# A cross network on one core: row products ordered from a table, sums that let tail reads pass, and a run that ends three tiles later in a split tile

## The chip, the cores and the metric

The kernel runs on one core of a Trainium2 chip. The metric is the time of one execution on the device, in microseconds. Before the change the median of three timed runs is 470.85 us (470.77 to 471.45).

## The reference

```python
B, F, D, L = 16384, 26, 16, 6          # Din = F * D = 416
x = x0                                  # (16384, 416), bfloat16
for l in range(L):
    proj = jnp.einsum('bd,de->be', x, ws[l]) + bs[l]
    x = x0 * proj + x                   # element by element
return x
```

Six layers follow each other. Each multiplies the batch with a 416 x 416 matrix, adds a bias, multiplies with the input x0 and adds its own input.

## The kernel before

**Tiling.** x is held transposed: features on the 128 partitions, batch along the free dimension. The batch of 16384 is cut into 8 groups (`g`) of 2048, a group into 4 chunks (`j`) of 512. The 416 features are three tiles of 128 (`t` as input, `i` as output) and a tail of 32. A *job* is a pair (g, l) of group and layer, 48 in all; `order` lists them so that several groups are under way at once. Work is put down in *items*: a "tile" is one output tile i of a job, for all four chunks; a "tails" item makes the 32 tail features of two or three jobs together (a *batch* of tails). A chunk of an output tile is one PSUM bank (128 x 512 in f32); there are eight banks, and `ring` holds the order in which they are handed out (`take`).

**Two forms of the same products.** A chunk of an output tile needs 3 x 128 + 32 rows of the contraction. `full` and `rows32` do that as three products over all 128 rows and one over a 32-row group. In the middle of the kernel, from item `s_lo` to `s_hi` (123 tiles, 14 batches of tails), `stream` does it otherwise: each 128-row product is cut into its four 32-row groups (`tile_position=(r * T32, 0)`), so that four products, on four row groups of the array and into four different banks, go side by side. A chunk then has 3 products on each row group and 1 more, its tail, on the group that `quad` gives: 13 in all, which is 13/4 of the array's time for one product. [...]

**What sets the order.** TensorE takes its queue in order, so the order of the row products decides how well the four row groups are filled. Before, `weave` finds it while the program is built: a beam search over states (when each row group is free, which chunks are in flight, when banks come free), with costs in units of one product: a hand-over 1.1, a bank back 1.1 + 2.85 + 0.8 after a chunk's last product, a tail read by VectorE 4.0, a change of array shape 0.45. At a batch of tails the row products stop, and `tails` is issued. Banks are taken from `ring` in turn (`held[c] = ring.pop(0)`). After the run the ring is turned to the rotation nearest to its state.

**Reading the banks.** `evacuate_chunk` has ScalarE add the bias and write a chunk to `tw` (L574). When both chunks of a pair are there, VectorE multiplies by x0 (L583) and adds the layer's input (L586), 1024 wide. `hold=True` and `release=True` let the recorder put a sum behind the next multiply, so that VectorE does not wait for itself. Of each batch of tails in the run, the second tail is read from PSUM by VectorE (L613), the others by ScalarE (L617); these are put down when `tails` is called, behind everything that VectorE's queue already holds. The tiles outside the run are read by `evacuate` (L539 on ScalarE, 1024 wide where two banks lie side by side; L548 and L553 on VectorE).

**Around the run.** The item ahead of the run is a full tile. The run ends ahead of tile 1 of job (6, 4), named `behind`; three more tiles, among them that one, follow in full form, in the modes FR and RF (first the full products and then the row products, or the other way), before the next batch of tails. The last job is made in natural layout (`nat_full`, L1122) and stored.

Of the kernel before, what the change touches and what calls it, by code (L numbers as in the profile page):

```python
# [3 lines left out]
P = 128  # L4
# [195 lines left out]
FENCE = 1.1  # L200
READ, SERVE, BACK = 1.1, 2.85, 0.8
SECOND = 4.0
CHANGE = 0.45


def weave(tails, events, width, slack=12):

    n = len(tails)
    size = [[3 + (r == tails[c]) for r in range(4)] for c in range(n)]
    rest = [[sum(size[c][r] for c in range(k, n)) for r in range(4)] for k in range(n + 1)]

    states = [(0.0, (0.0,) * 4, (), 0, (0.0,) * 4 + (4.6, 4.6, 9.3, 9.3), 8.5, 0, None, (0,) * 4)]
    for step in range(4 * n):  # L220
        found = {}
        for state in states:
            for due in (False, True):
                idle, free, flight, begun, banks, act, ev, log, last_ = state
                now = min(free)
                if due:
                    if ev == len(events) or begun < events[ev][0]:
                        continue
                    m = events[ev][1]
                    part = [(f - now + 1e-6) % 1.0 for f in free]  # L230
                    at = now + max(part)
                    if any((f - now + 1e-6) // 1.0 > v for f, v in zip(free, last_)):
                        continue
                    if len(banks) < m or any(banks[k] > at + 3 * k for k in range(m)):
                        continue
                    on = at + 3.25 * m + 3 * CHANGE
                    idle += sum(at - now - p for p in part)
                    moved = tuple(on + (f - now + 1e-6) // 1.0 for f in free)
                    flight = tuple((c, left, moved[r] if abs(end - free[r]) < 1e-9 else -9.0, r)
                                   for c, left, end, r in flight)  # L240
                    log = ((None, m, at, tuple(int((f - now + 1e-6) // 1.0) for f in free), on), log)
                    banks = list(banks[m:])
                    for k in range(m):
                        if k == 1:
                            banks.append(on - CHANGE - 1 + READ + SECOND + BACK)
                            continue
                        act = max(act, on - CHANGE - 1 + READ) + SERVE
                        banks.append(act + BACK)
                    banks = tuple(sorted(banks))
                    free, now, ev = moved, min(moved), ev + 1  # L250
                over = sorted((end, k) for k, (c, left, end, q) in enumerate(flight) if not left and end <= now)
                if over:
                    for end, k in over:
                        act = max(act, end + READ) + SERVE
                        banks += (act + BACK,)
                    banks = tuple(sorted(banks))
                    flight = tuple(f for f in flight if f[1] or f[2] > now)
                r = free.index(now)
                last = min(events[ev][0] + slack, n - 4) if ev < len(events) else n
                more = [(max(now, end + FENCE), k) for k, (c, left, end, q) in enumerate(flight) if left >> r & 1]  # L260
                if begun < last and banks:
                    more.append((max(now, banks[0]), None))
                if not more:
                    continue
                soon = min(s for s, k in more)
                for start, k in more:
                    if start > soon + 1.3:
                        continue
                    if k is None:
                        c, left = begun, 15  # L270
                    else:
                        c, left = flight[k][:2]
                    end = start + size[c][r]
                    left &= ~(1 << r)
                    fl = list(flight)
                    bk, sd = banks, begun
                    if k is None:
                        fl.append((c, left, end, r))
                        bk, sd = banks[1:], begun + 1
                    else:  # L280
                        fl[k] = (c, left, end, r)
                    fr = free[:r] + (end,) + free[r + 1:]
                    idl = idle + start - now
                    low = min(fr)
                    key = (tuple(round(10 * (f - low)) for f in fr),
                           tuple(sorted((lf, tails[x], max(-2, round(5 * (e - low)))) for x, lf, e, q in fl)),
                           sd, tuple(max(0, round(2 * (b - low))) for b in bk), ev)
                    if key not in found or found[key][0] > idl:
                        found[key] = (idl, fr, tuple(fl), sd, bk, act, ev, ((c, r, start, left), log),
                                      last_[:r] + (size[c][r],) + last_[r + 1:])  # L290

        def score(s):
            idl, fr, fl, sd = s[:4]
            own = list(rest[sd])
            age = 0
            far = 0.0
            for c, left, end, q in fl:
                age += sd - c
                chain = end
                for r in range(4):  # L300
                    if left >> r & 1:
                        own[r] += size[c][r]
                        chain += FENCE + size[c][r]
                far = max(far, chain)
            stop = max(f + w for f, w in zip(fr, own))
            return idl + 4 * max(stop, far) - sum(fr) - sum(own) + 0.15 * age + 0.5 * max(0, len(fl) - 6)

        states = sorted(found.values(), key=score)[:width]
        if not states:
            raise ValueError("no order found")  # L310
    best = min(states, key=lambda s: s[0] + 4 * max(s[1]) - sum(s[1]))
    log, entries = best[7], []
    while log:
        entries.append(log[0])
        log = log[1]
    out, latest, when = [], {}, 0
    for e in entries[::-1]:
        if e[0] is None:
            for r in range(4):
                for k in range(e[3][r]):  # L320
                    latest[r][-1 - k][0] = e[4] + e[3][r] - 1 - k
            out.append([e[2], -1, None, e[1]])
        else:
            c, r, start, left = e
            latest[r] = [[start + k, r, c, r] for k in range(size[c][r])]
            out += latest[r]
    out.sort(key=lambda x: (x[0], x[1]))
    return best[0] + 4 * max(best[1]) - sum(best[1]), max(best[1]), [(c, r) for t, o, c, r in out]


def bass_standalone__cross_network_dcn__recsys_kernel(
# [228 lines left out]
    tile_tw, tile_out = {}, {}  # L560

    def evacuate_chunk(g, l, i, j, b):
# [15 lines left out]
        a = j - j % 2  # L578
        if not {a, a + 1} <= out_:
# [3 lines left out]
        add("dve", lambda h: h.tensor_tensor(tw[r][:, o], tw[r][:, o], x0s[s0][:, c], ALU.mult),  # L583
            reads=[("tw", r, k) for k in both] + [x0_tok(s0, i, k) for k in both],
            writes=[("tw", r, k) for k in both], release=True)
        add("dve", lambda h: h.tensor_tensor(xs[so][:, c], tw[r][:, o], src(i, a, a + 2), ALU.add),  # L586
            reads=[("tw", r, k) for k in both] + [stok(i, k) for k in both],
            writes=[("x", so, i, k) for k in both], hold=True)
        if len(out_) == NJ:
            pr.flush()  # L590
            finish_tile(g, l)
# [94 lines left out]
    def tails(batch, corners_last=False):  # L686
        bs_ = take(len(batch))
# [13 lines left out]
        for (g, l), b in zip(batch, bs_):  # L701
# [21 lines left out]
        while later:  # L723
# [288 lines left out]
    def stream(run):  # L1012
# [10 lines left out]
        for c, r in order_:  # L1023
# [6 lines left out]
            if c not in held:  # L1030
                held[c], count[c] = ring.pop(0), 0
# [239 lines left out]
```

## Time and profile before

| | before |
|---|---|
| timed runs, median (lowest to highest) | 470.85 us (470.77 to 471.45) |
| profiled execution | 471.08 us |
| its span, first to last instruction | 469.3 us |
| TensorE clock granted | 1.000 of full speed |
| TensorE busy (PE) | 463.3 us, 7761 products |
| weight loads (PEld), beside PE | 268.9 us |
| VectorE (DVE) busy | 403.8 us, 700 instructions |
| ScalarE (ACT) busy | 378.8 us, 596 instructions |
| products in the run | 6396 (5904 from L1038 and 492 from L1042) |

A profile line gives the source line, the engine, the operation, what it writes and reads (output <- inputs), the shape, and the count; then busy time, mean length of one in ns, and the idle time of the engine just before, with what ended it. A timeline line gives the start and the length in us, and merges equal instructions that follow each other ("x12"): its length runs from the first start to the last end. Products overlap (each is shown from its start to its modelled end), so a group's busy time is less than count times length. PEld is TensorE's weight load, which stands in the same queue as the products.

### The profile page before, as it was taken

How to read it: one execution, taken by the hardware profiler on the slowest of the kernel's cores; microseconds unless marked ns; L12 is line 12 of the kernel's file. 1: busy time of each engine (PE TensorE's matmuls, PEld its weight loads, DVE VectorE, ACT ScalarE, POOL GpSimd, SP SyncE). 2: the span in 40 equal slices, each digit the busy share in tenths (PEclk: the TensorE clock that was granted, in tenths of full speed). 3: DMA queues.
4: the chain of work that ended last, by engine and by line, in shares of the span. 5: the costliest groups of instructions: out<-in, count | busy, mean ns of one | idle time of the engine just before them, and what ended most of it. 6: DMA issues, size and time to landing. Idle time of an engine off the chain costs nothing.

```text
span 469.3 us, 17315 instructions
## 1 busy us (share of the span) xinstructions
PE 463.3 (99%) x7761; PEld 268.9 (57%) x7761; DVE 403.8 (86%) x700; ACT 378.8 (81%) x596; POOL 7.3 (2%) x15
## 2 busy tenths in 40 slices
PE   9999999999999999999999999999999999999996
PEld 5444576665655557566666657565455665654442
DVE  2897988888889888988989899988989888988897
ACT  4687788787878788787988888888788887976775
POOL 1000000000000000000001000000000000000000
PEclk9999999999999999999999999999999999999999
DMA  8976878401002979094667993980000194128799
GB/s 224 187 158 129 157 130 168 64 3 26 2 3 40 175 187 148 20 150 148 115 114 114 235 150 71 177 252 3 25 2 3 26 147 148 36 48 185 153 170 290
DMA packets 139087, 53.75 MB, mean 115 GB/s; under 512 B 112763, under 2 KB 138501, under 8 KB 139013
## 3 DMA queue, kind: packets, MB, share of 16 engines
q1 hardware_dynamic: 138856, 52.54, 54.5%
q8 instruction: 60, 0.98, 0.9%
q14 instruction: 15, 0.11, 0.1%
q10 hardware_dynamic: 156, 0.11, 0.1%
HBM read 5.97 MB, written 13.63 MB: 42 GB/s over the span
## 4 chain that ended last, share of the span: by engine, by line
PE 93%; DVE 3%; ACT 1%; DMA 1%; issue 0%; DVEq 0%; ACTq 0%
PE ps L1038 68%; PE ps L659 7%; PE ps L1042 6%; PE ps L706 6%; PE ps L647 2%; PE ps L694 1%; DVE x L1186 1%; PE ps L680 1%; PE ps L778 1%; PE ps L796 1%; DVE x L1180 1%; DMA x<-x 1%; ACT tw L539 1%; DVE x L586 1%; DVE tw L583 1%; ACT tw L574 1%
## 5 line engine op out<-in xcount | busy, mean ns | idle before, releaser
L1038 PE MATMUL ps<-x,wm 32*128 32x512 bf16 x5904 | 353.2, 375 | 0.7 <-DVE ts L613 0.6
L574 ACT ACTIVATE tw<-ps,bias 128x512 bf16<-128x512 f32 x492 | 307.5, 687 | 41.5 <-PE ps L1038 26.4
L1038 PEld LDWEIGHTS ps<-x,wm 32*128 32x128 bf16 x5904 | 215.4, 92 | 125.1 <-PE ps L1038 3.4
L583 DVE TENSOR_TENSOR tw<-tw,x 128x1024 bf16<-128x1024 bf16 x246 | 167.4, 691 | 39.1 <-ACT tw L574 38.3
L586 DVE TENSOR_TENSOR x<-tw,x 128x1024 bf16<-128x1024 bf16 x246 | 159.6, 685 | 0.4
L1042 PE MATMUL ps<-x,w 32*128 32x512 bf16 x492 | 149.3, 374 | 0.0
L539 ACT ACTIVATE tw<-ps,bias 128x1024 bf16<-128x1024 f32 (+1 forms) x42 | 37.9, 970 | 15.2 <-PE ps L680 11.6
L1042 PEld LDWEIGHTS ps<-x,w 32*128 32x128 bf16 x492 | 42.3, 92 | 5.6
L659 PE MATMUL ps<-x,wm 128*128 128x512 bf16 x176 | 40.3, 380 | 0.0
L617 ACT ACTIVATE ts<-ps,bias 128x512 bf16<-128x512 f32 x33 | 21.0, 685 | 20.7 <-PE ps L694 20.7
L706 PE MATMUL ps<-x,wm 128*32 128x512 bf16 x564 | 33.6, 380 | 0.0
L548 DVE TENSOR_TENSOR tw<-tw,x 128x1024 bf16<-128x1024 bf16 (+1 forms) x39 | 24.3, 633 | 6.2 <-ACT tw L539 5.9
L659 PEld LDWEIGHTS ps<-x,wm 128*128 128x128 bf16 x176 | 16.2, 98 | 21.9 <-issue 3.6
L706 PEld LDWEIGHTS ps<-x,wm 128*32 128x32 bf16 x564 | 13.5, 96 | 17.6 <-ACT tw L574 3.2
L553 DVE TENSOR_TENSOR x<-tw,x 128x1024 bf16<-128x1024 bf16 (+1 forms) x39 | 23.1, 629 | 0.0
L621 DVE TENSOR_TENSOR x<-ts,x 128x512 bf16<-128x512 bf16 x47 | 18.3, 417 | 0.0
L613 DVE SCALAR_TENSOR_TENSOR ts<-ps,bias,x 128x512 bf16<-128x512 f32 x14 | 10.5, 749 | 6.3 <-PE ps L694 6.1
L619 DVE TENSOR_TENSOR ts<-ts,x 128x512 bf16<-128x512 bf16 x33 | 13.6, 416 | 0.0
L916 POOL COPY ost<-ot 128x512 bf16<-128x512 bf16 x6 | 5.9, 982 | 414.5 <-DMA ot<-x 414.5
L1122 PE MATMUL ps<-wm,x 128*128 128x416 bf16 x48 | 9.8, 340 | 0.0
L1174 ACT ACTIVATE x<-ps 128x416 bf16<-128x416 f32 x16 | 7.7, 517 | 2.1 <-PE ps L1122 2.0
L806 DVE COPY x<-ps 128x512 bf16<-128x512 bf16 x5 | 2.0, 422 | 8.3 <-PE ps L796 8.1
(50 smaller groups left out, 77.9 us busy)
## 6 DMA issues: line engine op xcount, KB each, us to landing
out_dram<-ost SPq DMA_DIRECT2D x6, 1664.0 KB, 7.9
x<-x SPq DMA_DIRECT2D x24, 96.0 KB, 2.2
x<-in_x_dram SPq DMA_DIRECT2D x8, 208.0 KB, 3.8
x<-in_x_dram SPq DMA_DIRECT2D x4, 416.0 KB, 7.8
out_dram<-ost SPq DMA_DIRECT2D x2, 832.0 KB, 5.4
wm<-in_ws_dram SPq DMA_DIRECT2D x5, 312.0 KB, 3.4
x<-x SPq DMA_DIRECT2D x22, 64.0 KB, 2.4
out_dram<-x SPq DMA_DIRECT2D x3, 416.0 KB, 4.4
```

Of the source, the lines that this page charges most:

```text
L539: add("act", lambda h, a=a, w=w, b0=b0: h.activation(tw[r][:, a * CH:(a + w) * CH], psum[:, b0 * CH:(b0 + w) * CH], ACT_F.Identity, bias=b ...
L548: add("dve", lambda h, a=a, e=e: h.tensor_tensor(tw[r][:, a * CH:e * CH], tw[r][:, a * CH:e * CH], x0s[s0][:, i * GC + a * CH:i * GC + e * ...
L553: add("dve", lambda h, a=a, e=e: h.tensor_tensor(xs[so][:, i * GC + a * CH:i * GC + e * CH], tw[r][:, a * CH:e * CH], src(i, a, e), ALU.ad ...
L574: add("act", lambda h: h.activation(tw[r][:, j * CH:(j + 1) * CH], bank(b), ACT_F.Identity, bias=bias[:, i, l:l + 1], scale=1.0), reads=[( ...
L583: add("dve", lambda h: h.tensor_tensor(tw[r][:, o], tw[r][:, o], x0s[s0][:, c], ALU.mult), reads=[("tw", r, k) for k in both] + [x0_tok(s0 ...
L586: add("dve", lambda h: h.tensor_tensor(xs[so][:, c], tw[r][:, o], src(i, a, a + 2), ALU.add), reads=[("tw", r, k) for k in both] + [stok(i ...
L617: add("act", lambda h: h.activation(ts[r][:, :], bank(b), ACT_F.Identity, bias=bias[:, 3, l:l + 1], scale=1.0), reads=[("ps", b), "bias"], ...
L621: add("dve", lambda h: h.tensor_tensor(x3s[so][:, :], ts[r][:, :], res, ALU.add), reads=[("ts", r)] + rtok, writes=[("x3", so), ("x3", so, ...
L659: add("pe", lambda h, t=t, j=j, k=k, w=w: h.matmul(bank(banks[j])[:, k * w:(k + 1) * w], wm[l][:, t, ecols], src(t, j, j + 1)[:, k * w:(k ...
L706: add("pe", lambda h, t=t, j=j, src=src, l=l, b=b, ro=ro, qo=qo: h.matmul(psum[qo, b * CH:(b + 1) * CH], wm[l][:, t, NT * P:D], src(t, j, ...
L1038: add("pe", lambda h, l=l, t=t, j=j, b=b, q=q, ecols=ecols, src=src, kw=kw: h.matmul(bank(b), wm[l][q, t, ecols], src(t, j, j + 1)[q, :], ...
L1042: add("pe", lambda h, l=l, b=b, q=q, ecols=ecols, s3=s3, kw=kw: h.matmul(bank(b), w3[l][q, ecols], s3[q, :], **kw), reads=tok3 + [("w3", l ...
```

## The change

1. **A table instead of the search.** `weave` is gone. `ORDER` is a string with one letter for each (chunk, row group) and a bar for each batch of tails; a letter says how many chunks ago the chunk was begun, and the row group. `replay` walks through it with its own costs (in twentieths of a product: hand-over 22, a bank back 70 after ScalarE's read begins, which is 19 after the last product's end, the next read 56 later, VectorE's tail bank 92, a change of shape 9), and from that fixes the start order of the single products, the bank of each chunk and the time at which each chunk is read. Bank numbers come from `replay`'s own list, which starts with banks 0 to 3 free at once, 4 and 5 at 92, 6 and 7 at 186, and no longer from `ring`.
2. **Sums yield.** `evacuate_chunk` makes two steps of a pair, `multiply` and `plus`. It keeps an estimate of when VectorE would be through (`dve`). If that lies past the end of the coming batch of tails (`phases`), the steps, and all that follow, go to `behind_tail`, and `tails` puts them down right after VectorE's own tail read, ahead of its work on the other tails.
3. **The run ends later.** `behind` is now tile 0 of job (7, 4), three tiles on, and belongs to the run. Of that last tile only the four tail products are row products in the run (`keep=NJ`, `part=0`); its twelve 128-row products follow right behind as full products, chunk by chunk, and each pair of chunks is read as soon as it is there. The other tiles keep their form.

```diff
-FENCE = 1.1
-READ, SERVE, BACK = 1.1, 2.85, 0.8
-SECOND = 4.0
-CHANGE = 0.45
-def weave(tails, events, width, slack=12):
...
+SLOT = 20
+FENCE, CHANGE = 22, 9
+READ, NEXT, BACK, SECOND, PAIR, TAILS = 19, 56, 70, 92, 56, 220
+LETTERS = "ABCDEFGHIJKLMNOPQRSTUVWXYZabcdefghijklmnopqrstuvwxyz0123456789"
+ORDER = (
+    "ABCDABaXOTUBCjUReLMhSHIVOTYBOIDhKAbJCQLVOEBXOQDNKADZOQXBOIDVCfMJSXYFOIDVCMXdSIHB|CXMRCPIBaDUZKTA"
...
+def replay(tails, events, keep, part):
...
+    size = [[(3 if c < n - keep else part) + (r == tails[c]) for r in range(4)] for c in range(n)]
+    free, flight, begun, act = [0] * 4, {}, 0, 170
+    banks = [(0, 0), (0, 1), (0, 2), (0, 3), (92, 4), (92, 5), (186, 6), (186, 7)]
...
+    for letter in ORDER:
+        if letter == "|":
...
+            for k, (_, b) in enumerate(got):
+                if k == 1:
+                    banks.append((on + SECOND, b))
                     continue
+                start = max(act, on - CHANGE + READ)
+                act = start + NEXT
+                banks.append((start + BACK, b))
...
+        age, r = divmod(LETTERS.index(letter), 4)
+        c, now = begun - age, free[r]
+        over(now)
+        if not age:
+            t, home[c] = banks.pop(0)
+            start, begun = max(now, t), begun + 1
+            flight[c] = [sum(1 << q for q in range(4) if size[c][q]), 0, r]
         else:
+            start = max(now, flight[c][1] + FENCE)
...
+        free[r] = start + SLOT * size[c][r]
...
     out.sort(key=lambda x: (x[0], x[1]))
...
-    def evacuate_chunk(g, l, i, j, b):
+    tile_tw, tile_out, ready = {}, {}, {}
+    phases, behind_tail, dve = [], [], [0]
+    def evacuate_chunk(g, l, i, j, b, read):
...
+        todo = [multiply, plus]
         if len(out_) == NJ:
-            pr.flush()
-            finish_tile(g, l)
+            todo.append(lambda: finish_tile(g, l))
+        while todo:
+            if behind_tail or phases and max(dve[0], ready[(g, l, i, a)]) + PAIR > phases[0] + 14:
+                behind_tail.extend(todo)
+                return
+            if len(todo) > 1 or len(out_) < NJ:
+                dve[0] = max(dve[0], ready[(g, l, i, a)]) + PAIR
+            todo.pop(0)()
...
-    def tails(batch, corners_last=False):
-        bs_ = take(len(batch))
+    def tails(batch, corners_last=False, banks=None):
+        bs_ = banks or take(len(batch))
...
                 evacuate_tail(*batch[k], bs_[k], vector=k == 1)
+                while behind_tail:
+                    behind_tail.pop(0)()
...
-    behind = ("tile", (LAST - 1, L - 2), 1)
+    behind = ("tile", (LAST, L - 2), 0)
...
-    def stream(run):
+    def stream(run, keep, part):
...
-            if c not in held:
-                held[c], count[c] = ring.pop(0), 0
...
-        at = list(ring)
-        turn = min(range(8), key=lambda k: max(at.index((k + i) % 8) - i for i in range(8)))
-        ring[:] = [(turn + i) % 8 for i in range(8)]
+        home = {c: b for _, r, c, b in plan if r >= 0}
+        ring[:] = sorted(left)
+        (g, l), i, _ = chunks[-1]
+        banks = [home[c] for c in range(len(chunks) - keep, len(chunks))]
...
+        full(g, l, i, banks, False, True, lambda j: j % 2 and evacuate(g, l, i, banks, [j - 1, j], 2),
+             ts_=range(part, NT))
+        ring.extend(sorted(banks))
...
-    s_lo, s_hi = items.index(("tile", (0, 2), 1)), items.index(behind)
+    s_lo, s_hi = items.index(("tile", (0, 2), 1)), items.index(behind) + 1
...
-            stream(items[s_lo:s_hi])
+            stream(items[s_lo:s_hi], NJ, 0)
```

More of the change, by code (lines that the diff above doesn't have):

```diff
@@ L197, in _ @@
                 run("dve", h)
-FENCE = 1.1
-READ, SERVE, BACK = 1.1, 2.85, 0.8
-SECOND = 4.0
-CHANGE = 0.45
-def weave(tails, events, width, slack=12):
-    n = len(tails)
[L216 to L263, printed above, removed]
-                    continue
[L265 to L322, printed above, removed]
-        else:
-            c, r, start, left = e
-            latest[r] = [[start + k, r, c, r] for k in range(size[c][r])]
-            out += latest[r]
@@ L327, in weave @@
     out.sort(key=lambda x: (x[0], x[1]))
-    return best[0] + 4 * max(best[1]) - sum(best[1]), max(best[1]), [(c, r) for t, o, c, r in out]
+    return out, read, [b for t, b in banks]
 def bass_standalone__cross_network_dcn__recsys_kernel(
@@ L578, in evacuate_chunk @@
         a = j - j % 2
+        ready[(g, l, i, a)] = max(ready.get((g, l, i, a), 0), read)
         if not {a, a + 1} <= out_:
@@ L582, in evacuate_chunk, with multiply, plus @@
         o, c = slice(a * CH, (a + 2) * CH), slice(i * GC + a * CH, i * GC + (a + 2) * CH)
[L583 to L588, printed above, removed]
-        if len(out_) == NJ:
-            pr.flush()
-            finish_tile(g, l)
+        def multiply():
+            add("dve", lambda h: h.tensor_tensor(tw[r][:, o], tw[r][:, o], x0s[s0][:, c], ALU.mult),
+                reads=[("tw", r, k) for k in both] + [x0_tok(s0, i, k) for k in both],
+                writes=[("tw", r, k) for k in both], release=True)
+        def plus():
+            add("dve", lambda h: h.tensor_tensor(xs[so][:, c], tw[r][:, o], src(i, a, a + 2), ALU.add),
+                reads=[("tw", r, k) for k in both] + [stok(i, k) for k in both],
+                writes=[("x", so, i, k) for k in both], hold=True)
+            if len(out_) == NJ:
+                pr.flush()
+        todo = [multiply, plus]
+        if len(out_) == NJ:
+            todo.append(lambda: finish_tile(g, l))
[6 more added lines that the diff above has]
+            todo.pop(0)()
     def evacuate_tail(g, l, b, vector=False):
@@ L1020, in stream @@
                 n += NJ
-        idle, end, order_ = weave([quad(g, l, j)[0] for (g, l), i, j in chunks], [(n, len(b)) for n, b in due], 400)
-        held, count, seen = {}, {}, {}
-        for c, r in order_:
-            if c is None:
-                tails(due.pop(0)[1], corners_last=True)
+        plan, read, left = replay([quad(g, l, j)[0] for (g, l), i, j in chunks], [len(b) for n, b in due],
+                                  keep, part)
+        phases.extend(on for _, r, _, on in plan if r < 0)
+        count, seen = {}, {}
+        for _, r, c, b in plan:
+            if r < 0:
+                dve[0] = max(dve[0], phases.pop(0)) + PAIR * len(behind_tail) + TAILS
+                tails(due.pop(0)[1], corners_last=True, banks=c)
                 continue
@@ L1029, in stream @@
                 start_job(g, l, ahead=False)
-            if c not in held:
-                held[c], count[c] = ring.pop(0), 0
-            b, q, ecols = held[c], slice(r * T32, (r + 1) * T32), slice(i * P, (i + 1) * P)
+            count[c] = count.get(c, 0) + 1
+            q, ecols = slice(r * T32, (r + 1) * T32), slice(i * P, (i + 1) * P)
             t = seen[c, r] = seen.get((c, r), -1) + 1
@@ L1035, in stream @@
             s3, tok3 = x3_src(g, l)
-            kw = dict(start=count[c] == 0, stop=count[c] == 4 * NT, tile_position=(r * T32, 0))
-            if t < NT:
+            kw = dict(start=count[c] == 1, stop=count[c] == 4 * NT + 1, tile_position=(r * T32, 0))
+            if t < (NT if c < len(chunks) - keep else part):
                 add("pe", lambda h, l=l, t=t, j=j, b=b, q=q, ecols=ecols, src=src, kw=kw: h.matmul(
```

68 lines of the change are left out of this document (62 added, 6 removed).

## The prediction

> **What bounds the kernel now.** I read the page's busy times first, then the chain that ended last, then the groups, and last the timeline at the run's two ends and across one batch of tail products.
>
> ```profile
> span 469.3 us, 17315 instructions
> PE 463.3 (99%) x7761; PEld 268.9 (57%) x7761; DVE 403.8 (86%) x700; ACT 378.8 (81%) x596; POOL 7.3 (2%) x15
> ...
> PE 93%; DVE 3%; ACT 1%; DMA 1%; issue 0%; DVEq 0%; ACTq 0%
> ```
>
> TensorE is busy for 99% of the span and carries 93% of the chain; VectorE and ScalarE have room. But "busy" hides something: in the run, four products on four 32-row groups of the array go side by side, and PE counts as busy when only one of them works. So the question is how many row-steps stand open.
>
> ```profile
> L1038 PE MATMUL ps<-x,wm 32*128 32x512 bf16 x5904 | 353.2, 375 | 0.7 <-DVE ts L613 0.6
> L574 ACT ACTIVATE tw<-ps,bias 128x512 bf16<-128x512 f32 x492 | 307.5, 687 | 41.5 <-PE ps L1038 26.4
> L583 DVE TENSOR_TENSOR tw<-tw,x 128x1024 bf16<-128x1024 bf16 x246 | 167.4, 691 | 39.1 <-ACT tw L574 38.3
> L586 DVE TENSOR_TENSOR x<-tw,x 128x1024 bf16<-128x1024 bf16 x246 | 159.6, 685 | 0.4
> L1042 PE MATMUL ps<-x,w 32*128 32x512 bf16 x492 | 149.3, 374 | 0.0
> L659 PE MATMUL ps<-x,wm 128*128 128x512 bf16 x176 | 40.3, 380 | 0.0
> L613 DVE SCALAR_TENSOR_TENSOR ts<-ps,bias,x 128x512 bf16<-128x512 f32 x14 | 10.5, 749 | 6.3 <-PE ps L694 6.1
> ```
>
> The end of the run, TensorE's timeline (start, length, what):
>
> ```profile
> 426.16 0.44 PE L1042 MATMUL ps<-x,w 32*128 32x512 bf16 x2
> 426.48 0.82 PE L1038 MATMUL ps<-x,wm 32*128 32x512 bf16 x3
> 427.14 0.37 PE L1042 MATMUL ps<-x,w 32*128 32x512 bf16 x1
> 427.44 2.76 PE L659 MATMUL ps<-x,wm 128*128 128x512 bf16 x12
> 430.14 0.61 PE L680 MATMUL ps<-x,w 32*128 32x512 bf16 x8
> 430.68 5.35 PE L659 MATMUL ps<-x,wm 128*128 128x512 bf16 x24
> ```
>
> Twelve full products take 2.76 us, the last of them 0.38, so one step is (2.76 - 0.38) / 11 = 0.216 us. A row product has the same 512 columns and the same step. The run's work is (5904 + 492) / 4 = 1599 steps, 345.4 us.
>
> One batch of tail products, again TensorE's timeline:
>
> ```profile
> 415.07 0.85 PE L1038 MATMUL ps<-x,wm 32*128 32x512 bf16 x10
> 415.85 2.12 PE L706 MATMUL ps<-x,wm 128*32 128x512 bf16 x36
> 417.91 0.42 PE L694 MATMUL ps<-x,w 32*32 32x512 bf16 x12
> 418.26 0.61 PE L1038 MATMUL ps<-x,wm 32*128 32x512 bf16 x7
> ```
>
> The last row product before it starts 0.375 before the end at 415.92, at 415.54, and has used its step by 415.76; the run goes on at 418.26. A batch takes 2.50 us, and there are 14 (L613, one a batch, has x14): 35.0 us. The new table has 14 bars, so this stays.
>
> The run's first rows, with ScalarE's reads beside them (the second of the two is shown once more by itself, from a narrower window):
>
> ```profile
> 37.86 2.76 PE L659 MATMUL ps<-x,wm 128*128 128x512 bf16 x12
> 40.23 2.12 ACT L539 ACTIVATE tw<-ps,bias 128x1024 bf16<-128x1024 f32 x2 [0.16 <-PE ps L659]
> ...
> 41.24 1.11 ACT L539 ACTIVATE tw<-ps,bias 128x1024 bf16<-128x1024 f32 x1
> ...
> 40.55 0.82 PE L1038 MATMUL ps<-x,wm 32*128 32x512 bf16 x12
> 41.21 0.38 PE L1042 MATMUL ps<-x,w 32*128 32x512 bf16 x4
> ```
>
> The run lasts from 40.55 to 427.14 + 0.22 = 427.36, 386.8 us. Less 345.4 of work and 35.0 of batches, **6.4 us stand open**. An order can win no more than that in the run.
>
> **The change part by part.**
>
> *Waits on VectorE's tail read.* After a batch VectorE reads one tail bank itself (L613). Twice it came to that late:
>
> ```profile
> 164.15 1.28 DVE L586 TENSOR_TENSOR x<-tw,x 128x1024 bf16<-128x1024 bf16 x2
> 165.31 0.54 PE L1038 MATMUL ps<-x,wm 32*128 32x512 bf16 x3
> 165.36 0.74 DVE L613 SCALAR_TENSOR_TENSOR ts<-ps,bias,x 128x512 bf16<-128x512 f32 x1
> 166.16 0.82 PE L1038 MATMUL ps<-x,wm 32*128 32x512 bf16 x9 [0.30 <-DVE ts L613]
> ...
> 330.79 0.37 PE L1038 MATMUL ps<-x,wm 32*128 32x512 bf16 x1
> 331.50 0.61 PE L1038 MATMUL ps<-x,wm 32*128 32x512 bf16 x8 [0.33 <-DVE ts L613]
> ```
>
> Two sums ran first (164.15), the read ended at 166.10, and no row issued anything until 166.16: the queue is in order, so one product without its bank stops all four rows. Against the usual 0.216 / 4 = 0.05 from product to product, the two places cost 0.63 and 0.66, together 1.3. In the new program multiply, sum and what follows are held until VectorE's tail read is queued, and all of the 1.3 goes: **-1.3** (0 if the read came late for another reason). What is late next there is ScalarE's two tail reads, which come at the same places in both.
>
> *Changes of array shape.* 12 full products from 427.44 are through at 427.44 + 12 x 0.216 = 430.03, the next shape starts at 430.14; its 8 (two steps) are through at 430.57, the next starts at 430.68. A change costs 0.10. Before, run, full, row, full and row pieces follow the run's end to the point where both programs meet (four changes); now the split tile's full products stand right behind the run and the row products after them (two): **-0.2**. The work is the same: a tile is 12 + 1 steps in either form, and the eight moved chunks and the split tile's tail rows are 26 + 1 steps in the run.
>
> *The run's end.* From 426.48 to 427.36 one row works alone, four steps: 0.88 x 3/4 = 0.66 open, counted with four rows. The new order ends with three products on one row: 0.65 x 3/4 = 0.49. **-0.2**.
>
> *The order itself.* Open time left is 6.4 - 1.3 - 0.7 = 4.4. A bank's next row group may start only after the one before has ended: 0.375 and a hop (0.06 in the VectorE wait above), 0.43 from start to start, which is 8 products of the queue (two steps). I counted, in the two built programs' instruction order, the hand-overs of a bank from one row to another with at most 8 products between the starts: 111 before, 24 after. With at most 9: 417 and 298. If the 4.4 follow the first count, 3.45 go; if the second, 1.26; none, if the open steps have other reasons. I see nothing that prefers one count, and take the middle: **-2.35**.
>
> ```profile
> PEld ps L1038 <- PE ps L1038: 3.4, 17, 0.5
> PEld ps L1122 <- DVE x L553: 0.4, 1, 0.4
> ```
>
> The first row (from the table of waits) shows such waits, 17 over 0.15 us. [...]
>
> *A new wait at the run's start.* The old code takes banks from the ring; counting its calls, the ring stands at 7, the full tile before the run fills banks 3, 4, 5, 6, and the old run opens on 7, 0, 1, 2. The new plan ignores the ring: it calls 0, 1, 2, 3 free at once and 4, 5, then 6, 7 later. Banks 3 and 4 are freed by the first of the two L539 reads from 40.23, banks 5 and 6 by the second. The second takes 1.11 and ends at 42.35; the first, as long, ends at 41.34. So the fourth product of the new run waits from 40.55 to 41.39, and the queue behind it with all rows: 0.84. Three steps later, at 42.05, the second wave wants bank 5, which the second read frees at 42.40: 0.35 more. **+1.2**. It is 0 only if the ring stood otherwise.
>
> *A new wait near the end.* Between its last two bars the new order reads a pair of x chunks (chunks 2 and 3 of input tile 2 of a layer-3 job) 42 products after the last product into its banks: 42 / 4 x 0.216 = 2.27 us. The chain between is a product's end 0.375, L574 0.687, L583 0.691, one other VectorE operation that the recorder puts between the pair's multiply and sum (some 0.60, as two L586 take 1.28), L586 0.685: 3.04, without hops or a turn in ScalarE's queue. So TensorE waits at least 0.8, and with one turn (0.60) 1.4: **+1.1**. Everything behind it on TensorE waits too. Apart from the run's first products, which read what the tiles before it made, the next pair is read 64 products after its last product, 3.5 us: enough.
>
> *Little or nothing.* Eight chunks are read 512 wide, not 1024 wide: 8 x 0.60 against 4 x 1.06, +0.6 on ScalarE, which has 19% free. SyncE issues group 4's load behind two rotations of tails; its first reader is many tiles later, and rotations behind it have a batch's time and more: 0. The first L1122 already waits for a VectorE sum (0.4, second row above), so some of the gain can stop there: 0 to 0.4, taken as **+0.2**.
>
> Sum: -1.3 - 0.2 - 0.2 - 2.35 + 1.2 + 1.1 + 0.2 = **-1.55 us**. The profiled execution took 471.08 with a span of 469.3; it should take 469.5. The median of the three timed runs is 0.23 lower, 470.85, so I say 469.3.
>
> **The rivals.**
>
> *No change: ScalarE sets the pace.* Then open steps only move.
>
> ```profile
> 419.51 3.00 ACT L574 ACTIVATE tw<-ps,bias 128x512 bf16<-128x512 f32 x5
> ```
>
> Five reads take 3.00, one (3.00 - 0.687) / 4 = 0.58. A chunk has 13 products, 13 / 4 x 0.216 = 0.70 of TensorE. ScalarE has to read 0.58 a chunk and two tails in 35 chunks, 0.62. And ScalarE idles 41.5 us before L574, released by TensorE. So it speaks against, but after a batch the reads come in bunches. Time: 470.85. [...]
>
> *Slower: the sums that yield come too late.* A held pair waits for the whole batch and the tail read behind it, up to 2.50 + 0.75 us. If its reader is near, TensorE stops as at the place above, after each of 14 batches. At 0.3 each that is 4.2: 473.5. It decides from 1.55 / 14 = 0.11 a batch. For it: VectorE at 86%. Against: in the new order only that one pair is read within 3.4 us of its last product.
>
> *More: the two new waits do not come.* Then -3.85: 467.0. That needs another ring and another VectorE order than I read.
>
> *It doesn't do what it says:* the open steps have other reasons than near hand-overs, 2.35 falls out, and +0.8 remains: 471.65 (0.17% above the median).
>
> **How the numbers follow.** Forecast 0.82, no change 0.06, late sums 0.04, no new waits 0.04, order without effect 0.04. Predicted: 469.3. The forecast's own bounds: by the first count -2.65 (468.2), by the second -0.46 (470.4). About 0.2% (0.94 us) is what a measurement of this kernel can tell; of the forecast's 0.82 some 0.04 lies inside it, towards the second count. Faster: 0.78 + 0.04 = 0.82. Same: 0.04 + 0.06 + 0.04 = 0.14. Slower: 0.04. The range 468.3 to 470.4 leaves out the rivals, 0.18, and a little of the low end.
>
> **What would show it.** Right: no wait on the vector tail read over 0.1; run and split tile in 386.8 - 345.4 - 35.0 = 6.4 down to about 5; a gap of 0.8 in the run's first wave with ScalarE's L539 as its end, one of 0.3 a wave later; one wait of about 1 us on VectorE's sum between the last two batches; two shape changes fewer. Wrong: ScalarE named before row products after most batches, or VectorE's sums named at many places.

## The result, and the profile after

The changed kernel takes 470.44 us (median of 20 runs, 469.85 to 471.0), the kernel before, timed beside it, 471.15 (20 runs, 470.68 to 471.67): ratio 0.9985 [0.9978, 0.9992], 0.71 us less. Forecast were 469.3 us and 1.55 less. The gain has the right sign and about half the size.

The page after, in the order in which the page before was read; behind it the instruction queue's row of the page before:

```profile
span 468.5 us, 17458 instructions
...
PE 460.2 (98%) x7827; PEld 259.6 (55%) x7833; DVE 402.9 (86%) x700; ACT 379.1 (81%) x605; POOL 7.6 (2%) x15
...
q8 instruction: 61, 1.00, 0.9%
...
PE 94%; DVE 3%; DMA 1%; ACT 1%; issue 0%; DVEq 0%; ACTq 0%
...
L1030 PE MATMUL ps<-x,wm 32*128 32x512 bf16 x6000 | 357.0, 374 | 1.5 <-DVE x L564 1.0
L547 ACT ACTIVATE tw<-ps,bias 128x512 bf16<-128x512 f32 x500 | 311.1, 688 | 48.0 <-PE ps L1030 38.0
...
L1034 PE MATMUL ps<-x,w 32*128 32x512 bf16 x504 | 149.1, 374 | 0.0
```

```profile
q8 instruction: 60, 0.98, 0.9%
```

L1030 and L1034 are the run's products (L1038 and L1042 before), L547 is ScalarE's read of a chunk (L574). Of PE, six records are missing; the weight loads are complete, and the marks below are taken from them: 7833, 72 more than before, one fetch of instructions more (61 for 60).

The run's beginning, its one wait on VectorE, and its end, from the changed kernel's timeline:

```profile
40.53 2.12 ACT L511 ACTIVATE tw<-ps,bias 128x1024 bf16<-128x1024 f32 x2 [0.16 <-PE ps L647]
...
40.85 0.10 PEld L1030 LDWEIGHTS ps<-x,wm 32*128 32x128 bf16 x3 [0.42 <-ACT tw L511]
...
41.70 0.82 PE L1030 MATMUL ps<-x,wm 32*128 32x512 bf16 x9 [0.45 <-ACT tw L511]
...
42.70 0.33 PEld L1030 LDWEIGHTS ps<-x,wm 32*128 32x128 bf16 x11 [0.46 <-ACT tw L511]
...
410.31 0.37 PE L1034 MATMUL ps<-x,w 32*128 32x512 bf16 x1
...
411.64 0.39 PE L1030 MATMUL ps<-x,wm 32*128 32x512 bf16 x4 [0.96 <-DVE x L564]
...
431.37 0.82 PE L1030 MATMUL ps<-x,wm 32*128 32x512 bf16 x3
...
432.11 2.27 PEld L647 LDWEIGHTS ps<-x,wm 128*128 128x128 bf16 x12 [0.42 <-issue]
```

Both forecast waits are there. Three products start, and the rest of the first wave waits for ScalarE's read (L511) until 41.70, 0.85 after the run's first weight load; a wave later there is a smaller wait of the same kind. From 410.31 to 411.64 all rows stand for the one pair's sum (L564), 1.28 over the usual 0.05. The run ends at 432.19 - 0.375 + 0.216 = 432.03 and so lasts 391.2 us. Its work is (6000 + 504) / 4 = 1626 steps of 0.216, 351.2; less 35.0 for the batches, 5.0 stand open (6.4 before).

Who waited for VectorE's tail read, before (first fence) and after (us in total, times):

```profile
  PEld ps L1038: 1.8, 3
  PE ps L1038: 0.6, 2
```

```profile
  PEld ps L1030: 0.3, 1
```

So the run did what was foreseen. The profiled execution took 470.27 with a span 0.82 shorter than before's. Four marks in the weight loads (the run's first, the last job's first, the kernel's last, the span's end) split the span:

| | run begins | run to last job | last job's products | last product to end | span |
|---|---|---|---|---|---|
| before | 40.55 | 411.78 | 11.94 | 5.01 | 469.28 |
| after | 40.85 | 410.10 | 11.99 | 5.52 | 468.46 |

From the run's first product to the last job 1.68 us are gained. 0.30 is lost ahead of the run, where nothing was changed; over all thirteen kernels here the run begins between 40.46 and 41.03. And 0.51 is lost behind TensorE's last product, where no line was changed either. There the transfers stand. The DMA view of the last stretch (448 to 470 us), before and after; an issue's last number is the median us from issue to landing:

```profile
q1 hardware_dynamic: 10569, 4.91, 90.3%
q10 hardware_dynamic: 144, 0.11, 1.4%
...
out_dram<-ost SPq DMA_DIRECT2D x2, 832.0 KB, 5.4
...
out_dram<-x ACTq DMA_DIRECT2D x1, 104.0 KB, 2.3
...
x<-x SPq DMA_TRANSPOSE x2, 3.4
```

```profile
q1 hardware_dynamic: 9516, 4.65, 85.5%
q10 hardware_dynamic: 144, 0.11, 1.5%
q8 instruction: 1, 0.02, 0.3%
...
out_dram<-ost SPq DMA_DIRECT2D x2, 832.0 KB, 6.7
...
out_dram<-x ACTq DMA_DIRECT2D x1, 104.0 KB, 2.5
...
x<-x SPq DMA_TRANSPOSE x2, 4.1
```

After, each kind shown here is slower, and one row is new: a fetch of instructions, 16 KB. The same view from 455.6 to 456.8 shows it alone:

```profile
q1 hardware_dynamic: 575, 0.39, 105.5%
q8 instruction: 1, 0.02, 5.3%
```

5.3% of 16 engines over 1.2 us is 1.02 us, the length of this one packet; beside it the packets of the other transfers (q1) come to 105.5% of the 16 engines' time. And VectorE, which before went through its natural-layout sums there without a gap, waits for the transpose:

```profile
457.97 0.59 DVE L1184 TENSOR_TENSOR x<-x,x 128x832 bf16<-128x832 bf16 x1 [0.26 <-DMA x<-x]
```

That transpose, the second one of x5 (the input of layer 5), stands on the chain that ended last in both kernels (start, length), before and after:

```profile
454.91 3.28 DMA x<-x
```

```profile
453.10 4.78 DMA x<-x
```

VectorE's last sum ends 2.19 us after TensorE's last weight load before and 2.47 after. That is 0.28 of the 0.51; the rest is in the stores behind it.

### The profile page after: what moved, and what is told of

Same layout as the page of the kernel before. It is cut to its first block, busy times and chain, and to the rows that moved or that the text cites. A ratio compares the mean times of both kernels' runs of the same rounds, so it can differ in the third digit from the quotient of the medians.

```text
span 468.5 us, 17458 instructions
## 1 busy us (share of the span) xinstructions
PE 460.2 (98%) x7827; PEld 259.6 (55%) x7833; DVE 402.9 (86%) x700; ACT 379.1 (81%) x605; POOL 7.6 (2%) x15
## 3 DMA queue, kind: packets, MB, share of 16 engines
HBM read 5.97 MB, written 13.63 MB: 42 GB/s over the span
## 4 chain that ended last, share of the span: by engine, by line
PE 94%; DVE 3%; DMA 1%; ACT 1%; issue 0%; DVEq 0%; ACTq 0%
PE ps L1030 69%; PE ps L694 7%; PE ps L1034 6%; PE ps L647 6%; PE ps L635 2%; PE ps L682 1%; DMA x<-x 1%; DVE x L1184 1%; PE ps L768 1%; PE ps L668 1%; DVE x L1178 1%; PE ps L786 1%; ACT tw L511 1%; DVE x L525 0%; DVE tw L520 0%
## 5 line engine op out<-in xcount | busy, mean ns | idle before, releaser
L1030 PE MATMUL ps<-x,wm 32*128 32x512 bf16 x6000 | 357.0, 374 | 1.5 <-DVE x L564 1.0
L547 ACT ACTIVATE tw<-ps,bias 128x512 bf16<-128x512 f32 x500 | 311.1, 688 | 48.0 <-PE ps L1030 38.0
L1030 PEld LDWEIGHTS ps<-x,wm 32*128 32x128 bf16 x6000 | 208.3, 92 | 134.3 <-ACT tw L547 3.2
L564 DVE TENSOR_TENSOR x<-tw,x 128x1024 bf16<-128x1024 bf16 x250 | 163.5, 688 | 0.5
L1034 PE MATMUL ps<-x,w 32*128 32x512 bf16 x504 | 149.1, 374 | 0.0
L1034 PEld LDWEIGHTS ps<-x,w 32*128 32x128 bf16 x504 | 41.7, 92 | 6.8 <-issue 0.2
L511 ACT ACTIVATE tw<-ps,bias 128x512 bf16<-128x512 f32 (+1 forms) x43 | 34.7, 879 | 12.5 <-PE ps L668 8.1
L647 PE MATMUL ps<-x,wm 128*128 128x512 bf16 x146 | 33.8, 382 | 0.9 <-issue 0.8
L520 DVE TENSOR_TENSOR tw<-tw,x 128x1024 bf16<-128x1024 bf16 (+1 forms) x35 | 21.6, 628 | 4.9 <-ACT tw L511 4.6
L647 PEld LDWEIGHTS ps<-x,wm 128*128 128x128 bf16 x152 | 14.0, 98 | 18.9 <-issue 3.4
L525 DVE TENSOR_TENSOR x<-tw,x 128x1024 bf16<-128x1024 bf16 (+1 forms) x35 | 20.6, 624 | 0.0
```

The lines of the kernel that those rows point to most:

```text
L511: add("act", lambda h, a=a, w=w, b0=b0: h.activation(tw[r][:, a * CH:(a + w) * CH], psum[:, b0 * CH:(b0 + w) * CH], ACT_F.Identity, bias=b ...
L520: add("dve", lambda h, a=a, e=e: h.tensor_tensor(tw[r][:, a * CH:e * CH], tw[r][:, a * CH:e * CH], x0s[s0][:, i * GC + a * CH:i * GC + e * ...
L525: add("dve", lambda h, a=a, e=e: h.tensor_tensor(xs[so][:, i * GC + a * CH:i * GC + e * CH], tw[r][:, a * CH:e * CH], src(i, a, e), ALU.ad ...
L547: add("act", lambda h: h.activation(tw[r][:, j * CH:(j + 1) * CH], bank(b), ACT_F.Identity, bias=bias[:, i, l:l + 1], scale=1.0), reads=[( ...
L647: add("pe", lambda h, t=t, j=j, k=k, w=w: h.matmul(bank(banks[j])[:, k * w:(k + 1) * w], wm[l][:, t, ecols], src(t, j, j + 1)[:, k * w:(k ...
L1030: add("pe", lambda h, l=l, t=t, j=j, b=b, q=q, ecols=ecols, src=src, kw=kw: h.matmul(bank(b), wm[l][q, t, ecols], src(t, j, j + 1)[q, :], ...
```

## The experiments

All were timed in five rounds beside the kernel before, whose median was 471.01 (e1 to e4), 471.16 (e6 to e9) and 471.11 (e10 to e12, on another chip than the other experiments). The changed kernel was timed beside 471.15, so where a median of e1 to e4 is set against it below, the difference is uncertain by 0.14 for that reason; the ratios are each to the kernel timed beside, and "run" is read within one execution. "Run" is the stretch from the run's first weight load to the last job's first; "end" is from the last weight load to the span's end; "fetch" is how many weight loads before the last one the last fetch of instructions begins, as the trace has it.

| | median us (lowest to highest) | ratio to before | run | end | fetch |
|---|---|---|---|---|---|
| before | 471.15 (470.68 to 471.67) | | 411.78 | 5.01 | 128 |
| after | 470.44 (469.85 to 471.0) | 0.9985 [0.9978, 0.9992] | 410.10 | 5.52 | 51 |
| e1_ring | 469.38 (469.22 to 469.91) | 0.997 [0.9959, 0.9981] | 409.36 | 5.97 | 58 |
| e2_noyield | 471.6 (470.95 to 472.19) | 1.0013 [1.0004, 1.0022] | 411.17 | 5.72 | 69 |
| e3_oldorder | 470.21 (469.68 to 470.54) | 0.9982 [0.9973, 0.9991] | 410.86 | 4.96 | 128 |
| e4_best | 468.89 (468.59 to 469.23) | 0.9958 [0.9945, 0.997] | 408.89 | 5.80 | 59 |
| e6_after60 | 469.68 (469.59 to 469.77) | 0.9968 [0.9955, 0.998] | 410.09 | 4.81 | 128 |
| e7_after16 | 470.07 (469.8 to 470.4) | 0.9973 [0.9963, 0.9983] | 410.10 | 5.78 | 71 |
| e8_before58 | 472.3 (471.82 to 472.5) | 1.0024 [1.0014, 1.0034] | 411.80 | 5.93 | 50 |
| e9_best60 | 467.91 (467.72 to 468.9) | 0.9934 [0.9922, 0.9947] | 408.77 | 4.56 | 128 |
| e10_ring60 | 468.29 (468.11 to 469.5) | 0.9944 [0.9932, 0.9957] | 409.28 | 4.44 | 128 |
| e11_noyield60 | 470.48 (470.07 to 471.15) | 0.9989 [0.998, 0.9997] | 411.24 | 4.75 | 128 |
| e12_pair60 | 468.79 (468.53 to 469.02) | 0.9949 [0.9935, 0.9962] | 409.53 | 4.55 | 128 |

**The parts of the change.** e1 gives the new plan the old ring's banks:

```diff
-    banks = [(0, 0), (0, 1), (0, 2), (0, 3), (92, 4), (92, 5), (186, 6), (186, 7)]
+    banks = [(t, first[k]) for k, t in enumerate((0, 0, 0, 0, 92, 92, 186, 186))]
...
-                                  keep, part)
+                                  keep, part, ring)
```

> The changed kernel, with its bank list taken from the ring as it stands when the run begins (7, 0, 1, 2 free, then 3, 4, then 5, 6) in place of 0 to 7. Theory 'wrong banks': the first wave of the changed kernel stops for 0.84 us on bank 3 and the second for 0.35 on bank 5, all four row groups behind them; with free banks both gaps go, the run is 0.8 to 1.2 us shorter than the changed kernel's, and if the end passes it on the time is lower by as much (ratio to the kernel before about 0.9965). Rival 'taken up elsewhere': a later wait (a bank, the late sum, the transfers of the last job) takes the time back; the run is less than 0.3 us shorter, or it is shorter and the time is not.

Measured: 1.06 under the changed kernel; the run is 0.74 shorter.

e2 takes the yielding away:

```diff
-            if behind_tail or phases and max(dve[0], ready[(g, l, i, a)]) + PAIR > phases[0] + 14:
+            if behind_tail:
```

> The changed kernel without the yielding of sums: multiplies and sums are put down at once, as before the change; order, banks and end as changed. Theory 'yield pays': with the new order VectorE comes late to its tail read at two to four of the 14 batches, TensorE waits 0.25 to 0.65 us there, and the kernel is 0.8 to 1.2 us slower than the changed one. Rival 'the order alone does it': the new order leaves VectorE free in time; no wait on the tail read over 0.15 us and the same time as the changed kernel.

Measured: 1.16 over the changed kernel; the run is 1.07 longer, and six weight loads (two to four were foreseen) and one product wait for VectorE's tail read, 2.0 and 0.3 us in all, where in the changed kernel one weight load does, 0.3.

e3 keeps the order and the run's end of the kernel before, written out as a table, so that only the yielding is new:

```diff
-    behind = ("tile", (LAST, L - 2), 0)
+    behind = ("tile", (LAST - 1, L - 2), 1)
...
+            if c not in held:
+                held[c] = ring.pop(0)
```

> The kernel before with one part of the change alone: the order of row products that the search found, written as a table, the run ending at its old place, banks in turn from the ring, and only the yielding of sums new. Theory 'yield pays': the two waits of 0.63 and 0.66 us on VectorE's tail read fall under 0.15 each, the run is 0.9 to 1.3 us shorter than before (385.5 to 385.9 in place of 386.8), its other open time stays. Rival 'replaced': ScalarE's tail reads or late sums take the place, and the run stays within 0.3 us of 386.8. Together with the changed kernel it tells what the new order itself brings: its run was shorter by 1.7, so the order and the end would bring about 2, less the new waits.

Measured: 0.8 under the kernel before timed beside it; the run is 0.92 shorter, and the end is as before (4.96). Three weight loads still wait for the tail read, 0.6 us in all.

e4 is e1, with the sum of the one pair that TensorE waited for put directly behind its multiply:

```diff
+        at_once = (g, l, i, a) == (LAST, 2, 2, 2)
...
-                writes=[("tw", r, k) for k in both], release=True)
+                writes=[("tw", r, k) for k in both], release=not at_once)
...
-                writes=[("x", so, i, k) for k in both], hold=True)
+                writes=[("x", so, i, k) for k in both], hold=not at_once)
```

> The changed kernel with the ring's banks (as e1_ring) and, for the one pair whose reader comes 42 products later, the sum put directly behind its multiply, not behind another pair's sum. Theory 'late sum': the wait of about 1.1 us between the last two batches falls by 0.5 (one VectorE operation less ahead of it), the run is 0.5 us shorter than in e1_ring. Rival: the reader then waits as long for something else, and the run is as in e1_ring. For the time: if all passes on, 1.3 to 1.7 us below the changed kernel; if the last job's transfers hold the end, about half of that.

Measured: 0.49 under e1, the run 0.47 shorter. In the runs of these four the waits of the forecast were all found; but the three with the new order kept the long end (5.7 to 6.0), and e3, with the old one, did not. What they share is the number of TensorE instructions: eight chunks moved into the run, of 13 products each in place of 4, make 72 products more. A piece of 16 KB is fetched about once in 128 products (60 for 7761, 61 for 7833). With 72 more the last piece is fetched not 128 products before the end but 50 to 70, among the last transposes and stores.

**The last fetch.** The test moves it and leaves the work as it is. `full` can issue a product of the jobs named in `HALVES` as two of half the columns (in both kernels the jobs named there lie in the run, so that it never does). e6, on the changed kernel:

```diff
-    HALVES = ((1, 2), (2, 1), (3, 0))
-    halves = [63]
+    HALVES = ((1, 0), (0, 1), (0, 2), (7, 5), (6, 5), (7, 4), (6, 4))
+    halves = [60]
```

> The changed kernel; 60 of the 512-column full products outside the run (36 ahead of it, 24 behind it, all before 440 us) are issued as two of 256 columns, so that TensorE does the same work with 60 more instruction pairs. Theory, the last instruction fetch: TensorE's instructions come by DMA in pieces of 16 KB, one per some 128 products; in the changed kernel the last piece is fetched 51 products before the end (455.7 us, 1.02 us on one DMA engine), in the middle of the last transposes and stores, in the kernel before it was 128 products before the end (446.9 us). With 60 products more it comes about 111 products before the end, near 447 us. Then the second x5 transpose takes about 3.3 us again (4.78 in the changed kernel), from the last product to the end 5.0 us (5.5), and the 60 splits cost at most 0.2: about 470.1, 0.3 below the changed kernel's 470.44. Rival, the end is late because of the new order itself (what VectorE and the stores still have open when the last products come): the fetch has no part in it, the transpose stays at 4.5 to 4.8 and the time is 470.4 to 470.6.

Measured: 0.76 under the changed kernel, and the two kernels' timed runs do not overlap; the theory had said 0.3, its rival 0. The run is as long as in the changed kernel (410.09 and 410.10), so the splits cost nothing there; the end is 4.81 for 5.52. The last stretch of its DMA view (448 to 470 us) has no row of q8, and the transfers are fast again:

```profile
q1 hardware_dynamic: 9357, 4.60, 79.5%
q10 hardware_dynamic: 144, 0.11, 1.4%
...
out_dram<-ost SPq DMA_DIRECT2D x2, 832.0 KB, 5.4
...
out_dram<-x ACTq DMA_DIRECT2D x1, 104.0 KB, 2.1
...
x<-x SPq DMA_TRANSPOSE x2, 3.3
```

e7 is the control, `halves = [16]`:

> The changed kernel with 16 products split in two, all ahead of the run: the control for the 60. Theory, the last fetch: it moves from 51 to about 67 products before the end, which is still among the transposes and stores (in the kernel without yielding it lay at 69, and its transpose took 4.5 to 5.0): the transpose stays above 4.3 us and the time is 470.4 to 470.5. Rival, the splits themselves help or hurt: a quarter of what the 60 do.

Measured: the end stays long (5.78), but the median is 0.37 under the changed kernel's, which neither theory had; 0.39 over e6. The 5.78 is from the slowest of the nine runs (470.4; the others took 469.8 to 470.16), so it need not hold for them. Where among the transfers the fetch falls may matter; that was not tested.

e8 is the kernel before with the same `HALVES` and `halves = [58]`:

> The kernel before with 58 products split in two outside the run, nothing else changed: same order, same waits in the run. Theory, the last fetch: one piece more is wanted, and it is fetched about 58 products before the end, near 454 us: the second x5 transpose goes from 3.28 to 4.5 or more, the stretch from the last product to the end from 5.0 to 5.5 or 5.8, and with 0 to 0.2 for the splits the time is 0.5 to 1.0 above the kernel before's 471.15, about 471.9. Rival, the end belongs to the order: 471.15 to 471.35.

Measured: 1.14 over the kernel before; the run is the same to 0.02, and the end 5.93 for 5.01. The theory had a slower transpose, and there it was wrong: here the last fetch begins at 457.7, behind the transposes, and only the stores are late:

```profile
q8 instruction: 1, 0.02, 0.4%
...
out_dram<-ost SPq DMA_DIRECT2D x2, 832.0 KB, 6.9
...
out_dram<-x ACTq DMA_DIRECT2D x1, 104.0 KB, 3.2
...
x<-x SPq DMA_TRANSPOSE x2, 3.4
```

This settles it: with the old order, and the same work in more instructions, the end is late; with the new order and the fetch moved, it is not. Nearly the same splits lengthen the end here and shorten it in e6, so the splits themselves are not the cause. And over the thirteen kernels of the table the end is 4.44 to 5.01 us where the last fetch begins 128 weight loads before the last one, and 5.52 to 5.97 where it begins 50 to 71 before it. VectorE is through 2.19 us after the last product in e8 as in before, so all of it is in the stores.

e9 is e4 with the 60 splits:

> e4 (the table's banks from the ring, and that one pair's sum directly behind its multiply) with the 60 splits of the first of these runs. Theory, the last fetch: from the last product to the end 5.0 us in place of 5.8, less 0 to 0.2 for the splits: 468.1 to 468.3 against 468.89. Rival, the end belongs to the order: 468.9 to 469.1.

Measured: 0.98 under e4, and the fastest kernel here, 0.9934 [0.9922, 0.9947] of before.

**The sizes, with the fetch out of the way.** e10 is e1, e11 is e2, and e12 the changed kernel with `at_once` alone, each with the 60 splits.

> e6 (the changed kernel with 60 products split) with the table's banks from the ring of the kernel before, so that the price of the new wait at the run's start is read with the last fetch out of the way. As the stretches of the profiles add up (from the run's first product to the last job's first, e1 is 0.74 shorter than the changed kernel): 468.95. The forecast's term of 1.2: 468.5. If the bank waits only move to later batches: 469.7.

> e6 with sums that do not yield to VectorE's tail read. By the profiles' stretches (1.07 longer than the changed kernel): 470.75. The forecast's term of 1.3: 471.0. If the yielding is worth nothing once the fetch is out of the way: 469.7.

> e6 with the sum of the one pair (chunks 2 and 3 of input tile 2 of the last group's layer 2) issued directly behind its multiply, as in e4, the banks as in the changed kernel. By the stretches (e4 is 0.47 shorter than e1): 469.2. The forecast's term of 1.1: 468.6. If the layer-3 job's products were held by something else as long: 469.7.

Measured against e6: e10 1.39 less (run 0.81 less), e11 0.80 more (run 1.15 more), e12 0.89 less (run 0.56 less). So e10 and e11 came out under the stretches' figure and the forecast's, e12 between the two. In e10 and e12 the medians fall by more than the run: the end, too, is 0.37 and 0.26 shorter, and why it varies by so much without a fetch in it stays open. The other chip alone is not the reason: e9, on e6's chip, has 4.56 too. In e12 TensorE still waits for that pair, though less:

```profile
410.25 0.37 PE L1036 MATMUL ps<-x,w 32*128 32x512 bf16 x1
...
411.10 0.40 PE L1032 MATMUL ps<-x,wm 32*128 32x512 bf16 x4 [0.48 <-DVE x L566]
```

## Why the prediction was wrong, point by point

*Waits on VectorE's tail read (-1.3).* The mechanism is right: 0.3 us at one place is left. Its worth is 0.92 of run with the old order (e3) and 1.07 and 1.15 with the new one (e2, e11); a little of what each wait gave up was lost again behind it.

*A new wait at the run's start (+1.2).* Place and cause are right, and the gap of 0.84 is there to 0.01, but the term was too large: the ring's banks gain 0.74 and 0.81 of run (e1, e10). The sum took the second gap of 0.35 as wholly new. The kernel before waits for ScalarE in its second wave too, 0.29 where the changed kernel has 0.46:

```profile
41.39 0.10 PEld L1038 LDWEIGHTS ps<-x,wm 32*128 32x128 bf16 x2 [0.29 <-ACT tw L539]
```

Laid beside e10, which has the same order, the changed kernel's 16th weight load of the run comes 0.83 later after the run's first, and its 48th 0.76 later.

*A new wait near the end (+1.1, bounds 0.8 to 1.4).* The one pair, at its place, 1.28. Removing the VectorE operation between multiply and sum brought 0.47 and 0.56 of run (e4, e12), since from 410.25 to 411.10 a wait of 0.80 over the usual 0.05 remains: the chain of reads was the longer part, as the sum had it.

*The order itself (-2.35), the run's end (-0.2) and the shapes (-0.2).* Only their sum can be read. The run of e9 is 3.01 shorter than before's. Of that the yielding has 0.92 to 1.15, and the pair's wait still costs 0.80 in it: 2.7 to 2.9 is left, against 2.75 forecast. The size is right; the reason given for it, fewer near hand-overs, is not shown. As their sign the forecast had the weight loads that wait over 0.15 us for the run's own products (3.4 us before). The rows of e3, with the old order, and of the changed kernel:

```profile
PEld ps L1031 <- PE ps L1031: 2.1, 10, 0.5
...
PEld ps L1031 <- PE ps L1035: 0.5, 3, 0.2
```

```profile
PEld ps L1030 <- PE ps L1030: 2.3, 15, 0.2
...
PEld ps L1030 <- PE ps L1034: 0.5, 3, 0.2
```

That is 2.6 and 2.8 us, and over all kernels with the new order it goes from 2.0 (e6) to 4.5 (e2): these rows do not fall with the order. Whether the gain lies in shorter hand-overs, which they leave out, or elsewhere stays open, and that the middle between the two counts came out is luck.

*The first L1122 (+0.2).* Not seen: from the point where both programs meet to the last job's first weight load both take 15.16 us.

So the run's sum holds: -1.55, or -1.75 without the last term, against -1.68 measured from the run's first product to the last job, and 5.0 us open where "about 5" stood. That it comes so near is in part luck: the yielding brought 0.2 to 0.4 less than its term, the start cost 0.4 to 0.5 less, the pair 0.2 more and the first L1122 0.2 less, and these cancel. *The rivals* fall with it: ScalarE did not hold the pace, as with eight reads of a chunk more the run went from 411.78 to 408.77 (e9); late sums appeared at one place and not at fourteen; and an order without effect would have left 0.4 of that 2.75.

*The step that failed* is the frame of the sum: it took what TensorE gains for what the kernel gains, and gave the stretch behind the last product no term. "The work is the same" is true of TensorE's time and not of its instructions. 72 products and 72 weight loads more moved the last fetch into the last transposes and stores, which without it are already the kernel's end. Taking the fetch out of there (e6) brings the kernel from 470.44 to 469.68 (the end of the profiled execution is 0.71 shorter), 1.48 us under the kernel before timed beside it; forecast were 1.55. Of the 1.14 by which 469.3 was too low, the fetch has 0.76, and 0.30 is the base: the three runs shown had a median of 470.85, twenty have 471.15. 0.08 is left. The time alone would have misled: 470.44 is what the forecast's second count of hand-overs gives (-0.46, 470.4), and only the marks in the span show that the run gained what was foreseen and the end lost it.

The page before already had the row (q8, 60 pieces, 0.9%), and the prediction does not mention it; 0.9% of the DMA engines' time and a 1% share of DMA in the chain look like nothing. Yet the place of one piece, the last, was worth 0.76 in the changed kernel (e6) and 1.14 in the kernel before (e8); what the others cost, if anything, no run here separates.

## What to carry to other kernels

Split the span at marks that both programs share before believing a total: here the run kept what was promised, and the loss stood in a stretch that no edit touched. This kernel ends in transfers that take 85 to 90% of the DMA engines' time (q1 from 448 to 470 us, after and before), and edits ahead of that which changed the number of TensorE instructions, 72 products more in the changed kernel and 58 split in two in e8, moved a fetch of 16 KB into them. Sixty products split in two, all before 440 us, moved it out and told at once that it was that (e6); sixteen did not move it out (e7). Where another kernel ends so, the same split is a cheap test.

## What the runs showed of the hardware

A fetch of instructions is one packet of 16,384 bytes, about once in 128 products (61 for 7833); where it was the late last one it took 1.02 us in the changed kernel, 1.32 in e8 and 1.57 in e7 (5.9% of 16 engines over 1.4 us, 4.9% over 2.0 us). Its harm was not its own length: the second x5 transpose went from 3.28 to 4.78 us from issue to landing, 1.5 us for a packet of 1.02, and the last store of 104 KB from 2.3 to 3.2 in e8. How one packet does that, the traces here don't show. And 60 products of 512 columns split into 120 of 256 cost nothing that can be read (the run in e6, of which 24 splits are a part, is 0.01 shorter than without).
